# Seven products in another order, with part of their factors' sums and two weight differences moved between them

## The chip, the core and the metric

The kernel runs on one core of one Trainium2 chip. TensorE does the matrix products into PSUM, VectorE, ScalarE and GpSimd do elementwise work, SyncE starts the DMA transfers; each engine works through its own queue in order and waits on semaphores. The metric is the device time of one execution in microseconds (us): 636.19 before, the median of 3 runs (636.09 to 636.86). The profiled execution spans 634.8 us.

## The reference

Two blocks follow one another. The first is a linear attention with a decaying state, the second a two-layer network with SiLU. Cut to what matters:

```python
# r, k, v, w: (4, 8, 768, 48); u: (8, 48)
for t in range(768):
    cur = u * k_t (outer) v_t
    y[:, :, t] = r_t @ (state + cur)
    state = w_t[..., None] * state + k_t (outer) v_t
x = y.transpose(0, 2, 1, 3).reshape(3072, 384)
h = x @ w_in                       # 384 -> 2048
out = (h * sigmoid(h)) @ w_out     # 2048 -> 384
```

All is float32 to the last, with the weights given in 64 bits and rounded on the chip.

## The kernel before

The 3072 tokens are 12 units of 256: 128 time steps of two batches at once. A unit goes through three stages. *Attention*: the decays are multiplied up over seven levels; at each level TensorE makes scores (`score_products`, L669), VectorE writes them into `score` through a mask (`keep_masked`, L679) and grows the queries (L607, L737), GpSimd the keys (L625, L634). The diagonal blocks of 8 steps are made apart: GpSimd multiplies (`block_bonus`, L487), VectorE sums (`block_sum`, L521), two transfers through DRAM turn them round (`block_move`), ScalarE copies them (`block_spread`, L548 and L550), VectorE shuffles (L551) and writes them into `score` (`block_write`, L557). *Up*: eight steps, each two products of 128 x 256 (`up`, L925) and one SiLU into `gt` (L934). *Down*: the second layer.

From unit 1 on the down stage is a Strassen product in its Winograd form. The result of a unit is cut into four quarters c11, c12, c21, c22 (batch by half of the 384 columns), the inner dimension of 2048 into two halves. Seven products of 128 x 1024 by 1024 x 192 (`quarter`, eight chunks each, L991) take the place of eight. Their left factors are `gt` itself or one of four sums s1 to s4 of quarters of `gt` (`sums`, L973, four pieces m = 0 to 3, four instructions each, into `quarters`, which lies in `temps`). Their right factors are quarters of w_out or one of four differences, made once for all units (`weight_sums`, L965: t1, t2, t3 in `own`, and b12 overwritten in `w_out_sb`). Each product ends in a PSUM tile `p_o`, of which there are two in turn; ScalarE copies the first (L998), VectorE adds each of the others to what is known (L1000), into `partial` (u1 to u4) or into the result (`ob`, whose first half lies in `temps`), and SyncE stores a batch of rows once both its halves are there.

The order of the work is written out by hand: the order of the calls is the order in each engine's queue. In the loop over i = 3 to 11, `mix(i)` gives thirteen groups of attention work of unit i (with the start of unit i + 1), and between them stand the steps of `downs(i - 2)` and `ups(i - 1)`, so many after each group as `ROOM` says: one product after each of the first three groups, two after the fourth, two after the fifth, then the up products. In the units after 3 the first three groups are nearly or wholly empty, so the seven products follow one another closely on TensorE, while VectorE and GpSimd work on the block sums, the keys and the queries. `sums` stands behind the up steps 5, 6 and 7. A product two places on needs the PSUM tile of this one, and so the add behind it.

Group 9 (from 0) of unit 3 holds the end of its scores, and in it `block_spread`, whose last instruction is VectorE's shuffle; group 10 holds what leads over to the next unit.

Of the kernel before, what the change touches and what calls it, by code (L numbers as in the profile page):

```python
# [15 lines left out]
ALU = mybir.AluOpType  # L16
# [22 lines left out]
def kernel(  # L39
# [11 lines left out]
    nc = tc.nc  # L51
# [271 lines left out]
    first = {}  # L323
# [10 lines left out]
    for b in range(NB):  # L334
        for x in range(2):
            nc.vector.tensor_single_scalar(out=own_mask[:, b, :, x:x + 1], in_=first[0], scalar=tok[:, x, b:b + 1],
                                           op=ALU.is_equal)
# [113 lines left out]
    at = 768  # L451
# [4 lines left out]
    block_both = spare[:, at:at + NB * H * BLK].rearrange("p (b h s) -> p b h s", b=NB, h=H)  # L456
# [89 lines left out]
    def block_spread(i):  # L546
        flat = block_both.rearrange("p b h s -> p b (h s)")
        nc.scalar.copy(out=flat[:, 0], in_=block_diag[0])  # L548
        for g in range(4):
            nc.scalar.copy(out=flat[(3 - g) * 32:(4 - g) * 32, 1], in_=block_diag[1][g * 32:(g + 1) * 32])  # L550
        nc.vector.stream_shuffle(out=flat[:, 1], in_=flat[:, 1], mask=list(range(31, -1, -1)))  # L551

    def block_write(i):

        shape = [128, NB, NP, L // BLK, BLK]
        for e in range(2):
            nc.vector.copy_predicated(out=score[:, i % NSC, e].rearrange("p (b q) (i s) -> p b q i s", b=NB, s=BLK),  # L557
                                      mask=block_mask[:, :, None].to_broadcast(shape),
                                      data=block_both[:, :, e::2][:, :, :, None, :].to_broadcast(shape))
# [301 lines left out]
    def both(fn, i, *args):  # L861
        return [(fn, i, b, *args) for b in range(NB)]
# [4 lines left out]
    def mix(i):  # L867

        first, second, later = i == NPAIR, i == NPAIR + 1, i > NPAIR
        ahead = i + 1 < len(units)  # L870

        def at(now, *steps):
            return steps if now else ()

        def bonus_steps(j, *steps):
            return [(block_bonus, j, x) for x in steps]

        def sum_steps(j, *steps):
            return [(block_sum, j, x) for x in steps]

        def turns(j):
            return [*both(turn, j, "w"), (product, j, 0), *both(turn, j, "k"), *both(turn, j, "r"), (grow_own, j, 0)]

        def start(j):
            return [*[(product, j, l) for l in range(1, NL)], (grow_own, j, 1)]

        early = bonus_steps(i + 1, 0, 1, 2, 3)
        middle = [*sum_steps(i + 1, 0, 1), *bonus_steps(i + 1, 4, 5)]
        move = [*sum_steps(i, 3, 4), (block_move, i), *at(ahead, (load_rk, i + 1))]
        groups = [[*at(first, *both(turn, i, "w"), (product, i, 0))],  # L890
                  [*at(first, *both(turn, i, "k"), *both(turn, i, "r"), (grow_own, i, 0))],
                  [*at(first, *start(i)), *at(second, *sum_steps(i, 0, 1), *bonus_steps(i, 4, 5))],
                  [(odd_keys, i, 2), (grow_keys, i, 2, False), (grow_queries, i, 2), *at(later, *sum_steps(i, 2))],
                  [(prepare, i, 3), *at(first, *bonus_steps(i, 0, 1, 2, 3)), *at(later, *bonus_steps(i, 6, 7))],
                  [(burst, i, 3), (keep_level, i, 3), *at(first, *sum_steps(i, 0, 1), *bonus_steps(i, 4, 5)), *at(later, *move)],
                  [(keep_level, i, 4), (go_on, i, 4), *at(first, (make_block_mask,), *sum_steps(i, 2), *bonus_steps(i, 6))],
                  [(prepare, i, 5), (reverse_v, i), *at(first, *bonus_steps(i, 7))],
                  [*at(first, *move), *at(later, (block_spread, i), (block_write, i))],
                  [(burst, i, 5), (keep_level, i, 5), *at(first, (block_spread, i)), (keep_level, i, 6), (go_on, i, 6),
                   *at(first, (block_write, i))],  # L900
                  [*at(later and ahead, *early)],
                  [*at(i < len(units) - NB, *both(turn_k, i)), *at(ahead, *turns(i + 1))],
                  [*both(y_state, i), *both(y, i), *both(update, i), *at(ahead, *start(i + 1)), *at(first, *early),
                   *at(later and ahead, *middle), (move_x, i)]]

        loads = block_loads(i + NSLOT) if i + NSLOT < len(units) else []
        if i + 1 < len(units):
            loads.insert(len(loads) // 2, (load_values, i + 1))

        behind = groups[3 if i > NTOK + 1 else 10:]  # L910
        for at, group in enumerate(behind):
            group += loads[at * len(loads) // len(behind):(at + 1) * len(loads) // len(behind)]
        return groups
# [3 lines left out]
    FH, DH = FC // 2, DM // 2  # L917
# [46 lines left out]
        out, one, two = ((t1, b12, b11), (t2, b22, t1), (t3, b22, b12), (b12, b21, t2))[which]  # L964
        nc.vector.tensor_tensor(out=out, in0=one, in1=two, op=ALU.subtract)  # L965

    def sums(i, m):

        lower, upper = (gt[i, x].rearrange("p a (b t) -> p b a t", b=NB) for x in (m, m + FH // 2))
        s1, s2, s3, s4 = (quarters[:, x, 2 * m:2 * m + 2, :] for x in range(4))  # L970
        for out, one, two, op in ((s1, lower[:, 1], upper[:, 1], ALU.add), (s2, s1, lower[:, 0], ALU.subtract),
                                  (s3, lower[:, 0], lower[:, 1], ALU.subtract), (s4, upper[:, 0], s2, ALU.subtract)):
            nc.vector.tensor_tensor(out=out, in0=one, in1=two, op=op)  # L973

    ob, partial = {}, {}
# [1 line left out]
    def quarter(i, which):  # L977

        n, b0 = units[i]

        def g(b, half):
            return lambda f: gt[i, (f + half * FH) // 2][:, f % 2, b * L:(b + 1) * L]

        def s(x):
            return lambda f: quarters[:, x, f, :]

        p = second[0].tile([128, DH], F32, name="p_o", bufs=2)

        left, right = ((g(0, 0), b11), (g(0, 1), b21), (s(1), t2), (s(2), t3), (s(0), t1), (g(1, 1), b12), (s(3), b22))[which]
        for f in range(FH):  # L990
            nc.tensor.matmul(p, lhsT=left(f), rhs=right[:, f, :], start=(f == 0), stop=(f == FH - 1))  # L991
        if which == 0:
            ob[i] = [out_room(b) for b in range(NB)]
            partial[i] = pt.tile([128, 4, DH], F32, name="partial", bufs=1)
        c11, c12, c21, c22 = (ob[i][x][:, y * DH:(y + 1) * DH] for x in range(2) for y in range(2))
        u1, u2, u3, u4 = (partial[i][:, x, :] for x in range(4))
        if which == 0:
            nc.scalar.copy(out=u1, in_=p)  # L998
        for to, known in ((), ((c11, u1),), ((u2, u1),), ((u3, u2),), ((c22, u3), (u4, u2)), ((c21, u3),), ((c12, u4),))[which]:
            nc.vector.tensor_tensor(out=to, in0=p, in1=known, op=ALU.add)  # L1000
        if which >= 5:
            b = 6 - which
            row0 = (b0 + b) * S + n * L
            nc.sync.dma_start(out=out[row0:row0 + L, :], in_=ob[i][b])

    def ups(i):

        steps = [[(up, i, m)] for m in range(FC // 2)]
        for m in range(FH // 2 - 1):

            steps[FH // 2 + 1 + m].append((sums, i, m))
        steps[-1].append((sums, i, FH // 2 - 1))
        return steps

    def downs(i):
        return [[(quarter, i, x)] for x in range(7)]

    def do(*steps):
        for fn, *args in steps:
            fn(*args)  # L1020
# [54 lines left out]
    for m in range(6):  # L1075
# [3 lines left out]

    blocks = block_loads(4)  # L1080
    do(*blocks[0:2], (level, 2, 2), (prepare, 2, 3), (weight_sums, 1), (down, 0, 1, 0), (down, 0, 0, 3), (down, 0, 1, 1),
       (sums, 1, 0), (bonus, 2, 0), (bonus_sum, 2, 0))
    do(blocks[2], (burst, 2, 3), (keep_level, 2, 3), (keep_level, 2, 4), (go_on, 2, 4), (prepare, 2, 5), (bonus, 2, 1),
       (bonus, 2, 2), (down, 0, 1, 2), (bonus_sum, 2, 1), (load_rk, 3), (load_u,), (sums, 1, 1), *blocks[3:7], (down, 0, 1, 3))
    do((burst, 2, 5), (keep_level, 2, 5), (keep_level, 2, 6), (go_on, 2, 6), (up, 1, 6), (bonus_spread, 2), (bonus_write, 2),
       (load_values, 3), *both(turn_k, 2), (weight_sums, 2), (up, 1, 7), (sums, 1, 2))
    do((sums, 1, 3), *both(y_state, 2), *both(y, 2), *both(update, 2),
       (move_x, 2),
       *blocks[7:])

# [2 lines left out]
    for i in range(3, len(units)):  # L1093
        steps = downs(i - 2) + ups(i - 1)
        groups = mix(i)
        if i == NTOK + 1:

            groups[3].insert(0, (weight_sums, 3))
        for group, room in zip(groups, ROOM):
            do(*group)  # L1100
            for step in steps[:room]:
                do(*step)
            steps = steps[room:]
# [32 lines left out]
```

## Time and profile before

| what | us | where it is from |
|---|---|---|
| time, median of 3 | 636.19 | the runs |
| up products, L925, TensorE busy | 258.1 | groups |
| the seven products, L991, TensorE busy (four groups) | 211.9 | groups |
| factor sums L973, VectorE busy (three largest groups) | 98.7 | groups by form |
| the weight difference L965, each | 2.2 | groups by form |
| adds L1000, each | 0.36 | groups by form |
| block writes L557, each | 1.75 | groups |

The 211.9 are 90.5 + 87.4 + 30.4 + 3.6, the 98.7 are 54.7 + 25.0 + 19.0. The columns of such a group are line, engine, operation, tiles, count, then busy time and mean ns of one, then the engine's idle time just ahead of them and who ended it.

The chain of work that ended last, by engine and line (how much of the span each takes on the path back from the last instruction):

```profile
PE 80%; POOL 9%; DMA 4%; DVE 3%; SPq 2%; issue 1%; ACT 1%; POOLq 0%; DVEq 0%; ACTq 0%
```

From 284.99 us on the pieces of this chain are TensorE's alone, one after the other.

### The profile page before, as it was taken

To read this page: it belongs to the slowest core of one execution; us is meant where nothing else is said; L and a number is where in the kernel's file an instruction comes from. 1 tells how busy PE (TensorE), PEld (TensorE's weight loads), DVE (VectorE), ACT (ScalarE), POOL (GpSimd) and SP (SyncE) were. 2 spreads that over 40 slices of the span, in tenths; PEclk is the share of its full clock that TensorE was granted. 3 is DMA by queue.
4 is the path that set the end of the run, shared out by engine and by line. 5 is a ranking of instruction groups with operands and counts; after the bars stand their busy time and mean duration, and the time that the engine had idled before them with its cause. 6 is when DMAs were issued, how large, how long until landed. Compare 5 with 4: busy or idle time off the path is not lost.

```text
span 634.8 us, 12253 instructions
## 1 busy us (share of the span) xinstructions
PE 620.5 (98%) x4574; PEld 561.6 (88%) x4574; DVE 434.4 (68%) x750; ACT 185.8 (29%) x377; POOL 373.7 (59%) x421
## 2 busy tenths in 40 slices
PE   8999999999888999999999999999999999999997
PEld 7888876889788899899889889989989989989997
DVE  7879779885593696696587596497597587561031
ACT  5798881202310321221221221221131122120120
POOL 6998298569469278478278378468458558500000
PEclk9999999999998999999999999999999999999999
DMA  9966864533353643543443442453353222100000
GB/s 216 290 152 167 190 176 50 112 73 65 81 71 55 128 65 52 126 64 51 111 67 52 110 72 49 96 87 51 79 102 53 47 62 52 34 0 26 26 1 25
DMA packets 203292, 53.75 MB, mean 85 GB/s; under 512 B 186465, under 2 KB 194657, under 8 KB 203233
## 3 DMA queue, kind: packets, MB, share of 16 engines
q1 hardware_dynamic: 201648, 52.39, 40.7%
q10 hardware_dynamic: 1584, 0.59, 0.5%
q8 instruction: 36, 0.59, 0.4%
q14 instruction: 24, 0.19, 0.1%
HBM read 43.67 MB, written 5.31 MB: 77 GB/s over the span
## 4 chain that ended last, share of the span: by engine, by line
PE 80%; POOL 9%; DMA 4%; DVE 3%; SPq 2%; issue 1%; ACT 1%; POOLq 0%; DVEq 0%; ACTq 0%
PE p_h L925 36%; PE p_o L991 27%; PE p_sc L669 4%; PE p_m L807 3%; PE p_m L947 2%; PE p_m L669 2%; PE p_m L794 2%; DMA tokens_w<-in_w_dram 2%; POOL ruk L487 2%; POOL tk L625 2%; POOL tw L408 2%; DMA u_bc<-in_u_dram 1%; POOL tk L634 1%; PE p_m L781 1%; PE p_sc L821 1%
## 5 line engine op out<-in xcount | busy, mean ns | idle before, releaser
L925 PE MATMUL p_h<-xt,w_in_sb 128*128 128x256 f32 x1152 | 258.1, 382 | 0.7 <-POOL tk L649 0.7
L925 PEld LDWEIGHTS p_h<-xt,w_in_sb 128*128 128x128 f32 x1152 | 215.9, 190 | 32.6 <-POOL tk L649 0.9
L934 ACT ACTIVATE gt<-p_h 128x512 f32<-128x512 f32 x90 | 53.6, 596 | 248.2 <-PE p_h L925 248.1
L625 POOL TENSOR_TENSOR tk<-tk,tw 128x256 f32<-128x256 f32 x126 | 86.9, 711 | 60.1 <-ACT tk L595 31.3
L991 PE MATMUL p_o<-own,temps 128*128 128x192 f32 x528 | 90.5, 331 | 5.8 <-DVE temps L1000 3.7
L991 PEld LDWEIGHTS p_o<-own,temps 128*128 128x128 f32 x528 | 87.6, 193 | 7.2 <-DVE temps L1000 4.6
L991 PE MATMUL p_o<-w_out_sb,gt 128*128 128x192 f32 x508 | 87.4, 328 | 0.0
L991 PEld LDWEIGHTS p_o<-w_out_sb,gt 128*128 128x128 f32 x508 | 82.7, 190 | 0.9 <-issue 0.4
L487 POOL TENSOR_TENSOR ruk<-tokens_rk 128x768 f32<-128x768 f32 (+1 forms) x36 | 56.3, 1574 | 39.4 <-DMA tokens_rk<-in_k_dram 28.2
L408 POOL TENSOR_TENSOR tw<-tw 128x256 f32<-128x256 f32 (+6 forms) x83 | 45.0, 542 | 52.2 <-DVE tw L360 48.3
L973 DVE TENSOR_TENSOR temps<-gt 128x256 f32<-128x256 f32 x84 | 54.7, 651 | 18.3 <-ACT gt L934 18.3
L595 ACT COPY tk<-tk 128x256 f32<-128x256 f32 x51 | 20.6, 403 | 101.6 <-POOL tk L625 71.9
L607 DVE TENSOR_TENSOR tr<-tr,tw 128x512 f32<-128x512 f32 x62 | 47.6, 768 | 3.7 <-POOL tk L625 1.1
L679 DVE COPY_PREDICATED score<-mask,p_sc 128x512 f32<-128x512 int8 x60 | 42.1, 753 | 10.9 <-PE p_sc L669 10.0
L669 PEld LDWEIGHTS p_sc<-tr,tk 48*128 48x128 f32 x496 | 30.4, 187 | 10.1 <-issue 6.6
L669 PE MATMUL p_sc<-tr,tk 48*128 48x128 f32 x496 | 36.5, 285 | 0.7 <-POOL tk L625 0.7
L521 DVE TENSOR_REDUCE block_sums<-ruk 128x4 f32<-128x192 f32 (+1 forms) x54 | 27.1, 542 | 7.5 <-POOL ruk L487 7.5
L1000 DVE TENSOR_TENSOR ob<-p_o,partial 128x192 f32<-128x192 f32 x22 | 7.9, 358 | 35.4 <-PE p_o L991 35.4
L1000 DVE TENSOR_TENSOR temps<-p_o,partial 128x192 f32<-128x192 f32 x22 | 7.9, 358 | 34.9 <-PE p_o L991 24.7
L557 DVE COPY_PREDICATED score<-spare 128x1024 f32<-128x1024 int8 x18 | 30.6, 1752 | 0.3
L991 PE MATMUL p_o<-w_out_sb,temps 128*128 128x192 f32 x176 | 30.4, 326 | 0.0
L487 POOL TENSOR_TENSOR tokens_rk<-tokens_rk,tokens_w 128x192 f32<-128x192 f32 (+1 forms) x36 | 29.4, 838 | 1.4
(170 smaller groups left out, 825.9 us busy)
## 6 DMA issues: line engine op xcount, KB each, us to landing
w_out_sb<-in_moe_w_in_dram SPq DMA_DIRECT2D x6, 768.0 KB, 8.1
tokens_rk<-in_r_dram SPq DMA_DIRECT2D x9, 384.0 KB, 4.5
tokens_rk<-in_k_dram SPq DMA_DIRECT2D x9, 384.0 KB, 5.5
tokens_w<-in_w_dram SPq DMA_DIRECT2D x9, 384.0 KB, 6.4
w_out_sb<-in_moe_w_out_dram SPq DMA_DIRECT2D x4, 768.0 KB, 6.8
own<-in_moe_w_out_dram SPq DMA_DIRECT2D x4, 768.0 KB, 5.2
xt<-yt SPq DMA_DIRECT2D x60, 48.0 KB, 2.0
raw<-in_w_dram SPq DMA_DIRECT2D x80, 32.0 KB, 2.4
```

The costliest lines, as they stand in the source:

```text
L408: engine.tensor_tensor(out=up, in0=t[:, :, 0::2], in1=t[:, :, 1::2], op=ALU.mult)
L487: mul = lambda out, one, two: nc.gpsimd.tensor_tensor(out=out, in0=one, in1=two, op=ALU.mult)
L521: add = lambda out, have: nc.vector.tensor_reduce(out=out, in_=have, axis=mybir.AxisListType.X, op=ALU.add)
L557: nc.vector.copy_predicated(out=score[:, i % NSC, e].rearrange("p (b q) (i s) -> p b q i s", b=NB, s=BLK), mask=block_mask[:, :, None].to_ ...
L607: nc.vector.tensor_tensor(out=odd, in0=odd, in1=tw[i][l][:, :, 0::2][:, :, :, None].to_broadcast([128, Q, L >> (l + 1), c]), op=ALU.mult)
L625: nc.gpsimd.tensor_tensor(out=out, in0=have, in1=odd_products(i, l, b, *blocks), op=ALU.mult)
L669: nc.tensor.matmul(bass.AP(tensor=s_p.tensor, offset=s_p.offset, ap=[s_p.ap[0], [apart * L // 2, 2], [1, L // 2]]), lhsT=tk[i][rows, X[l % ...
L679: nc.vector.copy_predicated(out=dst, mask=masks[l][:, :, None].to_broadcast([128, NB, NP, ni, c]), data=sc[e].rearrange("p (b q) (i c) -> ...
L925: nc.tensor.matmul(p_h[:, a, :], lhsT=w_in_sb[:, c, f * 128:(f + 1) * 128], rhs=xt[i][:, c, :], start=(c == 0), stop=(c == KC - 1))
L934: nc.scalar.activation(out=gt[i, m], in_=p_h, func=AF.Silu)
L973: nc.vector.tensor_tensor(out=out, in0=one, in1=two, op=op)
L991: nc.tensor.matmul(p, lhsT=left(f), rhs=right[:, f, :], start=(f == 0), stop=(f == FH - 1))
```

## The change

The products change places: after the two of `gt` itself and the one of s2 come s1, s4, s3 and last `gt` again. In the sums s1 and s2 stay behind the up steps (part 0). The four instructions that make s4 now stand behind the second product (part 1), the four that make s3 behind the third (part 2), since their products come only fifth and sixth. The weight difference t3 moves from the end of unit 2's stage into group 2 of pass 3, and the one that overwrites b12 from the head to the end of group 3. The adds go with the products: the fifth now makes c12 and the sixth two results, so the first batch's rows are stored behind the fifth product. Last, the shuffle moves from `block_spread` into `block_write`, and in unit 3 `block_write` from group 9 into group 10, so that both stand behind the mask writes and the first pair of factor sums. The aim is to ease VectorE's queue at the end of the up stage, and to have work in it done nearer to where it is needed.

```diff
--- before.py
+++ after.py
@@ -548,9 +548,11 @@
         nc.scalar.copy(out=flat[:, 0], in_=block_diag[0])
         for g in range(4):
             nc.scalar.copy(out=flat[(3 - g) * 32:(4 - g) * 32, 1], in_=block_diag[1][g * 32:(g + 1) * 32])
+
+    def block_write(i):
+
+        flat = block_both.rearrange("p b h s -> p b (h s)")
         nc.vector.stream_shuffle(out=flat[:, 1], in_=flat[:, 1], mask=list(range(31, -1, -1)))
-
-    def block_write(i):
 
         shape = [128, NB, NP, L // BLK, BLK]
         for e in range(2):
@@ -896,9 +898,8 @@
                   [(keep_level, i, 4), (go_on, i, 4), *at(first, (make_block_mask,), *sum_steps(i, 2), *bonus_steps(i, 6))],
                   [(prepare, i, 5), (reverse_v, i), *at(first, *bonus_steps(i, 7))],
                   [*at(first, *move), *at(later, (block_spread, i), (block_write, i))],
-                  [(burst, i, 5), (keep_level, i, 5), *at(first, (block_spread, i)), (keep_level, i, 6), (go_on, i, 6),
-                   *at(first, (block_write, i))],
-                  [*at(later and ahead, *early)],
+                  [(burst, i, 5), (keep_level, i, 5), *at(first, (block_spread, i)), (keep_level, i, 6), (go_on, i, 6)],
+                  [*at(later and ahead, *early), *at(first, (block_write, i))],
                   [*at(i < len(units) - NB, *both(turn_k, i)), *at(ahead, *turns(i + 1))],
                   [*both(y_state, i), *both(y, i), *both(update, i), *at(ahead, *start(i + 1)), *at(first, *early),
                    *at(later and ahead, *middle), (move_x, i)]]
@@ -964,12 +965,13 @@
         out, one, two = ((t1, b12, b11), (t2, b22, t1), (t3, b22, b12), (b12, b21, t2))[which]
         nc.vector.tensor_tensor(out=out, in0=one, in1=two, op=ALU.subtract)
 
-    def sums(i, m):
+    def sums(i, m, part):
 
         lower, upper = (gt[i, x].rearrange("p a (b t) -> p b a t", b=NB) for x in (m, m + FH // 2))
         s1, s2, s3, s4 = (quarters[:, x, 2 * m:2 * m + 2, :] for x in range(4))
-        for out, one, two, op in ((s1, lower[:, 1], upper[:, 1], ALU.add), (s2, s1, lower[:, 0], ALU.subtract),
-                                  (s3, lower[:, 0], lower[:, 1], ALU.subtract), (s4, upper[:, 0], s2, ALU.subtract)):
+        steps = ((s1, lower[:, 1], upper[:, 1], ALU.add), (s2, s1, lower[:, 0], ALU.subtract),
+                 (s4, upper[:, 0], s2, ALU.subtract), (s3, lower[:, 0], lower[:, 1], ALU.subtract))
+        for out, one, two, op in (steps[0:2], steps[2:3], steps[3:4])[part]:
             nc.vector.tensor_tensor(out=out, in0=one, in1=two, op=op)
 
     ob, partial = {}, {}
@@ -986,7 +988,7 @@
 
         p = second[0].tile([128, DH], F32, name="p_o", bufs=2)
 
-        left, right = ((g(0, 0), b11), (g(0, 1), b21), (s(1), t2), (s(2), t3), (s(0), t1), (g(1, 1), b12), (s(3), b22))[which]
+        left, right = ((g(0, 0), b11), (g(0, 1), b21), (s(1), t2), (s(0), t1), (s(3), b22), (s(2), t3), (g(1, 1), b12))[which]
         for f in range(FH):
             nc.tensor.matmul(p, lhsT=left(f), rhs=right[:, f, :], start=(f == 0), stop=(f == FH - 1))
         if which == 0:
@@ -996,10 +998,10 @@
         u1, u2, u3, u4 = (partial[i][:, x, :] for x in range(4))
         if which == 0:
             nc.scalar.copy(out=u1, in_=p)
-        for to, known in ((), ((c11, u1),), ((u2, u1),), ((u3, u2),), ((c22, u3), (u4, u2)), ((c21, u3),), ((c12, u4),))[which]:
+        for to, known in ((), ((c11, u1),), ((u2, u1),), ((u4, u2),), ((c12, u4),), ((u3, u2), (c22, u4)), ((c21, u3),))[which]:
             nc.vector.tensor_tensor(out=to, in0=p, in1=known, op=ALU.add)
-        if which >= 5:
-            b = 6 - which
+        if which in (4, 6):
+            b = which // 2 - 2
             row0 = (b0 + b) * S + n * L
             nc.sync.dma_start(out=out[row0:row0 + L, :], in_=ob[i][b])
 
@@ -1008,12 +1010,15 @@
         steps = [[(up, i, m)] for m in range(FC // 2)]
         for m in range(FH // 2 - 1):
 
-            steps[FH // 2 + 1 + m].append((sums, i, m))
-        steps[-1].append((sums, i, FH // 2 - 1))
+            steps[FH // 2 + 1 + m].append((sums, i, m, 0))
+        steps[-1].append((sums, i, FH // 2 - 1, 0))
         return steps
 
     def downs(i):
-        return [[(quarter, i, x)] for x in range(7)]
+        steps = [[(quarter, i, x)] for x in range(7)]
+        for part in 1, 2:
+            steps[part] += [(sums, i, m, part) for m in range(FH // 2)]
+        return steps
 
     def do(*steps):
         for fn, *args in steps:
@@ -1079,12 +1084,12 @@
 
     blocks = block_loads(4)
     do(*blocks[0:2], (level, 2, 2), (prepare, 2, 3), (weight_sums, 1), (down, 0, 1, 0), (down, 0, 0, 3), (down, 0, 1, 1),
-       (sums, 1, 0), (bonus, 2, 0), (bonus_sum, 2, 0))
+       (sums, 1, 0, 0), (bonus, 2, 0), (bonus_sum, 2, 0))
     do(blocks[2], (burst, 2, 3), (keep_level, 2, 3), (keep_level, 2, 4), (go_on, 2, 4), (prepare, 2, 5), (bonus, 2, 1),
-       (bonus, 2, 2), (down, 0, 1, 2), (bonus_sum, 2, 1), (load_rk, 3), (load_u,), (sums, 1, 1), *blocks[3:7], (down, 0, 1, 3))
+       (bonus, 2, 2), (down, 0, 1, 2), (bonus_sum, 2, 1), (load_rk, 3), (load_u,), (sums, 1, 1, 0), *blocks[3:7], (down, 0, 1, 3))
     do((burst, 2, 5), (keep_level, 2, 5), (keep_level, 2, 6), (go_on, 2, 6), (up, 1, 6), (bonus_spread, 2), (bonus_write, 2),
-       (load_values, 3), *both(turn_k, 2), (weight_sums, 2), (up, 1, 7), (sums, 1, 2))
-    do((sums, 1, 3), *both(y_state, 2), *both(y, 2), *both(update, 2),
+       (load_values, 3), *both(turn_k, 2), (up, 1, 7), (sums, 1, 2, 0))
+    do((sums, 1, 3, 0), *both(y_state, 2), *both(y, 2), *both(update, 2),
        (move_x, 2),
        *blocks[7:])
 
@@ -1095,7 +1100,8 @@
         groups = mix(i)
         if i == NTOK + 1:
 
-            groups[3].insert(0, (weight_sums, 3))
+            groups[2].append((weight_sums, 2))
+            groups[3].append((weight_sums, 3))
         for group, room in zip(groups, ROOM):
             do(*group)
             for step in steps[:room]:
```

## Prediction

> **What bounds the kernel now.** I read the busy shares first, then the chain of waits, then TensorE's timeline with its gaps, then VectorE and GpSimd side by side in one late pass. Below, "pass i" is one turn of the loop over i = 3 to 11, counted from the first of its seven products (P0 to P6, L991).
>
> ```profile
> PE 620.5 (98%) x4574; PEld 561.6 (88%) x4574; DVE 434.4 (68%) x750; ACT 185.8 (29%) x377; POOL 373.7 (59%) x421
> ```
>
> TensorE is busy 98% of the span and no matmul is removed, so only its gaps can be won. The table by stage, cut at each P0, says where they are:
>
> ```profile
> 128.01:180.26 52.25, 49.38 (x364) 45.16 (x361) 36.31 (x69) 10.88 (x24) 30.44 (x36) 1.00 0.40 73
> 180.26:235.46 55.20, 51.09 (x365) 46.89 (x361) 39.08 (x66) 10.79 (x24) 39.74 (x43) 0.97 0.48 82
> 333.73:382.47 48.74, 48.74 (x361) 45.29 (x361) 35.99 (x61) 10.78 (x24) 31.89 (x36) 1.00 0.43 77
> ```
>
> The first two numbers are the stage's length and TensorE's busy time. A late pass is pure TensorE, 48.74 us. Pass 3 is 3.5 us longer, pass 4 is 6.45 us longer, pass 5 (49.53) 0.8: 10.75 us in all. That is the most the change can bring. TensorE's timeline names the gaps (in brackets: idle, and who ended it):
>
> ```profile
> 137.35 5.47 PE L991 MATMUL p_o<-own,temps 128*128 128x192 f32 x32 [1.27 <-DVE temps L1000]
> 172.11 1.24 PE L781 MATMUL p_m<-ident,tk 128*128 128x128 f32 x8 [1.60 <-DVE score L679]
> 190.46 2.87 PE L991 MATMUL p_o<-own,temps 128*128 128x192 f32 x16 [2.00 <-DVE temps L1000]
> 195.43 4.55 PE L991 MATMUL p_o<-own,temps 128*128 128x192 f32 x16 [2.10 <-DVE partial L1000]
> ```
>
> p_o has two banks, so P(n+2) starts only when VectorE's add of P(n) (L1000) is out of its in-order queue. The 1.60 is another case: the mask write that frees p_m stands behind the shuffle L551, which idled 4.83 us for a copy that waits for a transfer.
>
> Now pass 7, P0 at 333.66, VectorE:
>
> ```profile
> 331.13 1.25 DVE L973 TENSOR_TENSOR temps<-gt 128x256 f32<-128x256 f32 x1
> 332.42 1.15 DVE L973 TENSOR_TENSOR temps<-temps,gt 128x256 f32<-128x256 f32 x1
> 333.49 0.83 DVE L973 TENSOR_TENSOR temps<-gt 128x256 f32<-128x256 f32 x1
> 335.32 0.42 DVE L973 TENSOR_TENSOR temps<-temps,gt 128x256 f32<-128x256 f32 x1
> ...
> 339.63 0.36 DVE L1000 TENSOR_TENSOR temps<-p_o,partial 128x192 f32<-128x192 f32 x1
> 341.76 0.36 DVE L1000 TENSOR_TENSOR partial<-p_o,partial 128x192 f32<-128x192 f32 x1 [1.77 <-PE p_o L991]
> 342.04 0.91 DVE L607 TENSOR_TENSOR tr<-tr,tw 128x512 f32<-128x512 f32 x1
> 342.87 1.12 DVE L521 TENSOR_REDUCE block_sums<-ruk 128x4 f32<-128x192 f32 x4
> 344.36 0.36 DVE L1000 TENSOR_TENSOR partial<-p_o,partial 128x192 f32<-128x192 f32 x1 [0.37 <-PE p_o L991]
> ```
>
> and GpSimd in the same stretch:
>
> ```profile
> 330.62 2.66 POOL L826 TENSOR_TENSOR state<-state,tw 128x512 f32<-128x512 f32 x2
> 333.25 2.91 POOL L408 TENSOR_TENSOR tw<-tw 128x256 f32<-128x256 f32 x6
> 336.12 1.61 POOL L634 TENSOR_TENSOR tk<-tk,tw 128x256 f32<-128x256 f32 x2
> 339.22 1.96 POOL L487 TENSOR_TENSOR ruk<-tokens_rk 128x384 f32<-128x384 f32 x2 [1.49 <-DVE block_sums L521]
> 341.15 0.59 POOL L487 TENSOR_TENSOR tokens_w<-tokens_w 128x192 f32<-128x192 f32 x1
> 341.81 2.14 POOL L487 TENSOR_TENSOR tokens_rk<-tokens_rk,tokens_w 128x192 f32<-128x192 f32 x3
> 343.91 2.61 POOL L625 TENSOR_TENSOR tk<-tk,tw 128x256 f32<-128x256 f32 x4
> 346.48 1.82 POOL L487 TENSOR_TENSOR spare<-tokens_rk 128x768 f32<-128x768 f32 x1
> ```
>
> The same factor sum L973 takes 0.42 us beside an idle GpSimd, and 1.25, 1.15, 0.83 beside L826 and L408: it ends when the GpSimd instruction ends. The L1000 adds, which read PSUM, take 345 to 359 ns whatever GpSimd does. From 339.22 on GpSimd runs without a gap until after P6.
>
> **The Trainium skill.** "SBUF — State Buffer", Who interferes with whom: a VectorE instruction with two SBUF inputs takes the read port that GpSimd uses, and the later one waits for the whole other instruction; reductions never contend. The trace agrees (1.25 against 0.42; L1000 constant). "VectorE: DVE Perf Modes", the errata section: an fp32 tensor_tensor takes (N+151)/0.96 ns, 424 for N = 256; the trace has 0.42, and 0.34 start to start. "Perfetto Trace Analysis", GPSIMD Engine Instruction: trust start-to-start spacing, so I take 0.65 for an L625 (2.61/4) and 0.6 for the short L487.
>
> **The change, part by part.**
>
> *Removed.* Nothing; every instruction is still there. *Moved:* of 16 factor sums (L973) 8 stay with the up products. The four s4 go behind the add of P1, the four s3 behind the add of P2, both ahead of the adds that free the banks of P2 and P3. In pass 3 two weight differences (L965, 1.7 us apart from contention) come in too, ahead of the same adds.
>
> *Before P0.* VectorE is rid of 1.4 us ahead of the transposes (4 x 0.34) and as much ahead of the state add. In late passes this is hidden: the state add waits for TensorE's update (end at P0) and the first add for P1. It moves GpSimd forward: the transposes start 1.3 us sooner, the state products L826 wait for TensorE at about 330.2, so L487 starts near 337.2 instead of 339.2, the block sums being done by then.
>
> *Shuffle and write in pass 3.* The mask write follows its predecessor at 166.2 and ends by 167.5, before TensorE's L781 is due at 170.5: the 1.60 us goes. The shuffle still waits for the transfer, with one pair of sums and the transposes of the next unit queued behind it; GpSimd waits for those, which costs pass 4, not pass 3.
>
> *Passes 5 to 10, the term that decides.* P1 ends at 338.9 in pass 7's clock, and P5 is due at 346.7. Between them VectorE now has: add 0.3, four s4, add 0.3, four s3, L607, L521 (1.05), add 0.35. Bound below, no contention: 0.3 + 1.36 + 0.3 + 1.36 + 0.65 + 1.05 + 0.35 = 5.4 us, fits into 7.8. But each of the nine two-input instructions meets a running GpSimd instruction. In the alternation at 333 to 335 a sum's cycle is GpSimd's step plus about 0.1, so 0.7 each: eight take 5.6. Step by step: the first s4 waits for the short L487 until 339.7, s4 ends at 342.05, add 342.35, s3 pairs with the four L625 and ends at 345.0; L607 then meets the long L487 (1.82) and ends near 347.1, the reduce at 348.1, the add at 348.4. P5 starts 1.7 us late. If GpSimd stands one instruction later, L607 pairs with the last L625 and the wait is 0.15; one earlier, 2.2. I take 1.7. P4 (due 344.1) is not late, s3 and s4 are in time for P5 and P4. Six passes: 6 x 1.7 = 10.2, less the 0.8 that pass 5 lost before: +9.4.
>
> *Pass 11* has no L826 ahead, so GpSimd is done sooner with the short ones: I get 0.3.
>
> *Pass 3.* TensorE from P0 at 128.0: first add at 133.75 (it stood at 136.94), so the 1.27 goes. Then s4 2.1 beside L408, L607 0.75, weight difference 2.0 with the wait: second add done at 139.25, P4 due at 138.55, 0.75 late. Then s3 2.6, L607 1.0, the other difference 2.2: third add done at 145.35, P5 due at 141.9, 3.45 late. 4.2 against 1.55 before: +2.7 (uncontended: 0.65 to 2.05, no change).
>
> *Pass 4.* Relative to P0 GpSimd is ahead by 2 us, but s4 now meets two 1.8 us L487 before the first block sums; the second add ends 3.4 late, and s3 with L607 adds 2.9: 6.3 against 6.45 before, -0.1 (uncontended 2.35, which would be -4.1).
>
> *Tail.* After 592 GpSimd is idle and VectorE nearly so; moving sums there costs nothing. The order of output rows changes one transfer each; the last is still after P6.
>
> Sum: +2.7 - 1.6 - 0.1 + 9.4 + 0.3 = **+10.7 us, 647**.
>
> **Rivals.**
> 1. *Stalls of the early passes go, late ones stay hidden.* For it: the uncontended sums fit in every late pass with over 2 us to spare. Against: GpSimd's unbroken row. Pass 3 -0.2, L781 -1.6, pass 4 -4.1, pass 5 -0.8: -6.7, 629.5.
> 2. *Lucky pairing.* Late passes lose 0.15: +2.7 - 1.6 - 0.1 + 0.9 - 0.8 + 0.3 = +1.4, 637.6. My margin on GpSimd's position is only 0.1 to 0.2 us, so it is real; but nine pairings must all stay.
> 3. *Worse pairing*, 2.2 a pass and 0.5 more in pass 3: +14.2, 650.4.
>
> **How the numbers follow.** Forecast 0.52, rival 1 0.22, rival 2 0.12, rival 3 0.14. Range: from rival 1's time to somewhat over rival 3's, 630 to 651.5. Within 0.2% (634.9 to 637.5) about half of rival 2 and a little of rival 1: 0.08; faster 0.20; slower 0.72.
>
> **What would show it.** In the changed profile each late pass is about 50.4 us between P0s, with TensorE's gap at P5 put down to the L1000 add of "partial", and L973 showing means well over 0.42 between P1 and P3. L781 has no gap in pass 3. I am wrong if the s3 after P2 run at 0.34 apart, or if GpSimd's row has holes there; then rival 1 holds.

## The result, and the profile after

The change makes the kernel slower: 654.14 us (median of 4, 653.87 to 656.3) against 636.53 (median of 4 runs of the kernel before), a ratio of 1.0284 (95% interval 1.0261 to 1.0308). The forecast was 647.0 with a range of 630.0 to 651.5: the direction was right, but the loss is 17.6 us against 10.7, and the time lies above the range. The profiled execution is the slowest of the four (span 654.5 us, 19.7 more than before).

From the page after, the busy shares of the engines and the chain that ended last:

```profile
PE 627.8 (96%) x4574; PEld 566.8 (87%) x4574; DVE 469.6 (72%) x750; ACT 186.2 (28%) x377; POOL 377.2 (58%) x421
PE 69%; DVE 18%; POOL 4%; issue 4%; DMA 3%; ACT 2%; SPq 0%; POOLq 0%; DVEq 0%; ACTq 0%
```

VectorE holds 18% of the path to the end where it held 3%. TensorE's own waits, of which there had been several kinds, are now nearly one line (engine, line, who ended the wait: us in total, times, longest):

```profile
PE p_o L993 <- DVE partial L1002: 19.9, 10, 3.2
```

L993 and L1002 are the products and the adds, L991 and L1000 before; the sums L973 are now L975, the query growth L607 is L609, the keys L625 are L627, the up products L925 are L926 and their SiLU L934 is L935. The stages, cut at each P0, for passes 3, 4, 7 and 8 (columns as in the prediction):

```profile
128.18:182.61 54.43, 51.23 (x362) 46.94 (x361) 40.62 (x71) 10.64 (x24) 34.64 (x38) 0.97 0.37 70
182.61:237.81 55.20, 50.96 (x364) 46.91 (x361) 43.19 (x62) 10.78 (x24) 38.47 (x40) 0.97 0.48 82
...
341.73:392.70 50.97, 49.02 (x365) 45.27 (x361) 39.78 (x60) 10.87 (x24) 31.72 (x36) 1.00 0.41 74
392.70:445.34 52.64, 50.69 (x364) 46.94 (x360) 39.77 (x60) 10.88 (x24) 31.71 (x36) 0.97 0.40 72
```

Pass 7 was 48.74 and is 50.97. Pass 8 is 1.67 longer still, and its granted clock (third column from the end) is 0.97. All passes beside what was forecast, in us longer than before:

| pass | 3 | 4 | 5 | 6 | 7 | 8 | 9 | 10 | 11 | sum |
|---|---|---|---|---|---|---|---|---|---|---|
| forecast | +1.1 | -0.1 | +0.9 | +1.7 | +1.7 | +1.7 | +1.7 | +1.7 | +0.3 | +10.7 |
| measured | +2.18 | 0.00 | +3.42 | +2.23 | +2.23 | +3.89 | +2.21 | +2.24 | +1.16 | +19.56 |

Ahead of pass 3 it is 0.17 more, and the tail is 0.03 shorter, which makes the 19.7. Now VectorE in pass 7, between the add of P1 and that of P3:

```profile
347.29 0.36 DVE L1002 TENSOR_TENSOR temps<-p_o,partial 128x192 f32<-128x192 f32 x1 [2.22 <-issue]
347.57 2.62 DVE L975 TENSOR_TENSOR temps<-gt,temps 128x256 f32<-128x256 f32 x4
350.11 0.34 DVE L1002 TENSOR_TENSOR partial<-p_o,partial 128x192 f32<-128x192 f32 x1
350.38 2.99 DVE L975 TENSOR_TENSOR temps<-gt 128x256 f32<-128x256 f32 x4
353.29 2.30 DVE L609 TENSOR_TENSOR tr<-tr,tw 128x512 f32<-128x512 f32 x1
355.51 1.12 DVE L521 TENSOR_REDUCE block_sums<-ruk 128x4 f32<-128x192 f32 x4
356.56 0.34 DVE L1002 TENSOR_TENSOR partial<-p_o,partial 128x192 f32<-128x192 f32 x1
```

GpSimd beside it:

```profile
349.87 3.21 POOL L627 TENSOR_TENSOR tk<-tk,tw 128x256 f32<-128x256 f32 x4
353.05 1.99 POOL L487 TENSOR_TENSOR spare<-tokens_rk 128x768 f32<-128x768 f32 x1
```

and TensorE's P5 behind it, in pass 7 and in pass 8:

```profile
356.95 2.87 PE L993 MATMUL p_o<-own,temps 128*128 128x192 f32 x16 [1.96 <-DVE partial L1002]
...
407.92 4.55 PE L993 MATMUL p_o<-own,temps 128*128 128x192 f32 x16 [1.96 <-DVE partial L1002]
```

This is the chain of the prediction: the four s4 take 2.62 and the four s3 2.99 where 1.4 each would do alone; the four L627 are stretched from 2.61 to 3.21; L609 meets the long L487 and takes 2.30 where it took 0.91; the add of P3 ends at 356.90, and P5 starts at 356.95. In pass 8 the same gap is followed by 3.41 us in which TensorE runs at half clock, so the same 16 matmuls take 4.55 instead of 2.87.

### The profile page after: what moved, and what is told of

It is laid out like the page before. It is cut to its first block, busy times and chain, and to the rows that moved or that the text cites. A ratio compares the mean times of both kernels' runs of the same rounds, so it can differ in the third digit from the quotient of the medians.

```text
span 654.5 us, 12253 instructions
## 1 busy us (share of the span) xinstructions
PE 627.8 (96%) x4574; PEld 566.8 (87%) x4574; DVE 469.6 (72%) x750; ACT 186.2 (28%) x377; POOL 377.2 (58%) x421
## 4 chain that ended last, share of the span: by engine, by line
PE 69%; DVE 18%; POOL 4%; issue 4%; DMA 3%; ACT 2%; SPq 0%; POOLq 0%; DVEq 0%; ACTq 0%
PE p_h L926 35%; PE p_o L993 16%; DVE temps L975 7%; PE p_sc L671 4%; DVE tr L609 4%; DVE block_sums L521 3%; PE p_m L809 3%; PE p_m L796 2%; PE p_m L948 2%; PE p_m L671 2%; POOL tk L627 1%; DMA tokens_w<-in_w_dram 1%; DMA raw<-in_k_dram 1%; DVE partial L1002 1%; PE p_m L783 1%
## 5 line engine op out<-in xcount | busy, mean ns | idle before, releaser
L926 PE MATMUL p_h<-xt,w_in_sb 128*128 128x256 f32 x1152 | 258.2, 382 | 1.0 <-POOL tk L651 0.7
L926 PEld LDWEIGHTS p_h<-xt,w_in_sb 128*128 128x128 f32 x1152 | 215.9, 190 | 33.1 <-POOL tk L651 0.9
L627 POOL TENSOR_TENSOR tk<-tk,tw 128x256 f32<-128x256 f32 x126 | 92.8, 757 | 79.7 <-PE p_sc L671 41.1
L935 ACT ACTIVATE gt<-p_h 128x512 f32<-128x512 f32 x90 | 53.6, 596 | 259.4 <-PE p_h L926 259.3
L993 PE MATMUL p_o<-own,temps 128*128 128x192 f32 x528 | 95.1, 339 | 16.8 <-DVE partial L1002 16.8
L993 PEld LDWEIGHTS p_o<-own,temps 128*128 128x128 f32 x528 | 90.5, 198 | 19.4 <-DVE partial L1002 19.4
L993 PE MATMUL p_o<-w_out_sb,gt 128*128 128x192 f32 x508 | 87.6, 329 | 0.0
L993 PEld LDWEIGHTS p_o<-w_out_sb,gt 128*128 128x128 f32 x508 | 83.1, 191 | 0.9 <-issue 0.4
L487 POOL TENSOR_TENSOR ruk<-tokens_rk 128x768 f32<-128x768 f32 (+1 forms) x36 | 52.9, 1481 | 44.7 <-DMA tokens_rk<-in_k_dram 21.2
L975 DVE TENSOR_TENSOR temps<-gt 128x256 f32<-128x256 f32 x84 | 61.6, 763 | 22.2 <-ACT gt L935 22.2
L408 POOL TENSOR_TENSOR tw<-tw 128x256 f32<-128x256 f32 (+6 forms) x83 | 41.7, 503 | 37.8 <-DVE tw L360 33.9
L609 DVE TENSOR_TENSOR tr<-tr,tw 128x512 f32<-128x512 f32 x62 | 55.7, 898 | 3.7 <-POOL tk L627 1.1
L681 DVE COPY_PREDICATED score<-mask,p_sc 128x512 f32<-128x512 int8 x60 | 42.0, 753 | 11.5 <-PE p_sc L671 10.7
L993 PE MATMUL p_o<-w_out_sb,temps 128*128 128x192 f32 x176 | 32.3, 339 | 3.3 <-DVE partial L1002 3.2
L993 PEld LDWEIGHTS p_o<-w_out_sb,temps 128*128 128x128 f32 x176 | 30.5, 199 | 3.9 <-DVE partial L1002 3.9
L636 POOL TENSOR_TENSOR tk<-tk,tw 128x256 f32<-128x256 f32 x36 | 32.8, 932 | 0.5
L487 POOL TENSOR_TENSOR tokens_rk<-tokens_rk,tokens_w 128x192 f32<-128x192 f32 (+1 forms) x36 | 31.0, 881 | 1.4
L1002 DVE TENSOR_TENSOR temps<-p_o,partial 128x192 f32<-128x192 f32 x22 | 7.9, 358 | 31.7 <-PE p_o L993 15.8
```

The costliest lines, as they stand in the source:

```text
L408: engine.tensor_tensor(out=up, in0=t[:, :, 0::2], in1=t[:, :, 1::2], op=ALU.mult)
L487: mul = lambda out, one, two: nc.gpsimd.tensor_tensor(out=out, in0=one, in1=two, op=ALU.mult)
L609: nc.vector.tensor_tensor(out=odd, in0=odd, in1=tw[i][l][:, :, 0::2][:, :, :, None].to_broadcast([128, Q, L >> (l + 1), c]), op=ALU.mult)
L627: nc.gpsimd.tensor_tensor(out=out, in0=have, in1=odd_products(i, l, b, *blocks), op=ALU.mult)
L636: nc.gpsimd.tensor_tensor(out=have, in0=have, in1=odd_products(i, l, b, [2, NP * ni]), op=ALU.mult)
L681: nc.vector.copy_predicated(out=dst, mask=masks[l][:, :, None].to_broadcast([128, NB, NP, ni, c]), data=sc[e].rearrange("p (b q) (i c) -> ...
```

## The experiments

In what follows a "gap" is taken from one matmul's start to the next, less the 0.16 us that lie between two starts when nothing waits, so that P5's gap in pass 7 reads 2.12 (1.96 in the brackets of the lines above).

**The order alone** (e1_order: the kernel before, with the new order, its adds and its stores; of the edit the order is shown).

```diff
-((g(0, 0), b11), (g(0, 1), b21), (s(1), t2), (s(2), t3), (s(0), t1), (g(1, 1), b12), (s(3), b22))
+((g(0, 0), b11), (g(0, 1), b21), (s(1), t2), (s(0), t1), (s(3), b22), (s(2), t3), (g(1, 1), b12))
```

> The kernel before with the products in the new order and the adds and stores that go with it, nothing else moved. If the loss comes from sums that meet GpSimd between P1 and P5, the order by itself costs nothing: late passes 48.7 us, all in all 636.5 within 1. If the new order itself is to blame (the adds, two results behind P5, the store behind P4), most of the 17 us is here: 645 to 654.

636.24 us, ratio 1.0004 (0.9996 to 1.0012); passes 6 to 9 are 48.74, without a gap. The order costs nothing.

**The shuffle and write alone** (e2_shuffle, on the kernel before; the shuffle's own move, as in the change, is not shown).

```diff
-[(burst, i, 5), (keep_level, i, 5), *at(first, (block_spread, i)), (keep_level, i, 6), (go_on, i, 6),
- *at(first, (block_write, i))],
-[*at(later and ahead, *early)],
+[(burst, i, 5), (keep_level, i, 5), *at(first, (block_spread, i)), (keep_level, i, 6), (go_on, i, 6)],
+[*at(later and ahead, *early), *at(first, (block_write, i))],
```

> The kernel before with the shuffle and write of the block sums moved, nothing else. The 1.60 us ahead of L781 in pass 3 goes. The transposes of the next unit come some 3 us sooner on VectorE, so GpSimd is sooner in pass 4 too and its 6.4 us of stalls shrink by up to as much again: 632 to 635. Rival: pass 4 waits for GpSimd at the same absolute time, and the 1.6 is given back there: 636.5.

636.37 us, 1.0007 (0.9997 to 1.0017). Pass 3 is 50.85 (it was 52.25), pass 4 53.52 (55.20), pass 5 53.72 (49.53). Both savings are there and are given back one pass later than the rival said: in pass 5 a gap of 3.2, with 3.4 us of half clock behind it.

**s3 back behind the up steps** (e3_s3_back, on the changed kernel, as are the next ones).

```diff
-            steps[FH // 2 + 1 + m].append((sums, i, m, 0))
-        steps[-1].append((sums, i, FH // 2 - 1, 0))
+            steps[FH // 2 + 1 + m] += [(sums, i, m, x) for x in (0, 2)]
+        steps[-1] += [(sums, i, FH // 2 - 1, x) for x in (0, 2)]
...
-        for part in 1, 2:
-            steps[part] += [(sums, i, m, part) for m in range(FH // 2)]
+        steps[1] += [(sums, i, m, 1) for m in range(FH // 2)]
```

> The changed kernel with s3 back behind the up steps; s4 stays behind P1. If the add of P3 is late because s3 and L609 stand ahead of it and take turns with GpSimd, it is now in time: no gap at P5 in passes 6 to 11, stages of 48.7 us, and 631 to 638 in all. If the order, the weight differences or the shuffle are to blame, over 645.

635.53 us, 0.999 (0.9984 to 0.9997). There is no gap in passes 6 to 11, which are as long as before (48.74, and 47.15 for 10 and 11). VectorE in pass 7 (P0 at 332.34):

```profile
341.57 0.82 DVE L609 TENSOR_TENSOR tr<-tr,tw 128x512 f32<-128x512 f32 x1
...
343.35 0.34 DVE L1002 TENSOR_TENSOR partial<-p_o,partial 128x192 f32<-128x192 f32 x1
```

The add of P3 comes 11.0 us after P0 instead of 14.8. Taking the four s3 away from this place undoes the whole loss.

**s4 back, s3 left where the change puts it** (e4_s4_back: the same edit with 0 and 1 in the up steps, part 2 behind P2).

> The changed kernel with s4 back behind the up steps; s3 stays behind P2. If it is only the amount of work between P1 and P5, half of the sums are gone and so is most of the gap (0 to 0.5 us a pass, 637 to 642). If it is the taking of turns, GpSimd, held up less by s4, reaches its long product (L487, 1.8 us) sooner, one of the s3 or L609 meets it all the same, and the gap at P5 stays at 1.5 to 2.2 us in passes 5 to 10: 647 to 653.

640.16 us, 1.0064 (1.0048 to 1.008), gaps at P5 of 0.45 to 0.79 in passes 6 to 10. That is the number of the first reading, a little over its 0 to 0.5, and I had the second one for mine. VectorE in pass 7:

```profile
341.16 3.11 DVE L975 TENSOR_TENSOR temps<-gt 128x256 f32<-128x256 f32 x4
344.19 1.13 DVE L609 TENSOR_TENSOR tr<-tr,tw 128x512 f32<-128x512 f32 x1
```

and GpSimd's long product:

```profile
345.78 1.81 POOL L487 TENSOR_TENSOR spare<-tokens_rk 128x768 f32<-128x768 f32 x1
```

The s3 are as slow as ever (3.11 for four), so they do take turns; but L609 is done in 1.13, since GpSimd reached its long L487 only at 345.78. I had expected it sooner. With the s4 back ahead of them, VectorE comes later to the first block sums, and GpSimd waits 1.49 us for these. So this run does not tell the two readings apart by its time. The next two do.

**Without the long L487** (e6_no_long, bonus step 6).

```diff
-        else:
+        elif step == 7:
             e = step - 6
```

> The changed kernel without the multiply of block bonus step 6 (GpSimd's 1.8 us L487 behind the four L627), so part of the scores is left out. If the query growth L609 behind s3 takes 2.30 us because it stands beside just that instruction, it now takes 0.7 to 0.9 and the gap at P5 falls from 2.1 to 0.5 to 0.8 in passes 5 to 10: 642 to 646. If the gap comes from VectorE's own work or from the adds, it stays at 2 and the time at 652 or more.

643.31 us, 1.0103 (1.0082 to 1.0124); P5's gap is 0.49 to 0.50 in passes 6 to 10 (2.12 with it), and none in pass 11. VectorE in pass 7:

```profile
350.25 0.68 DVE L609 TENSOR_TENSOR tr<-tr,tw 128x512 f32<-128x512 f32 x1
```

One GpSimd instruction that meets one VectorE instruction is worth 1.6 us of each of passes 6 to 10: L609 takes 0.68 and not 2.30, and the gap is 0.50 and not 2.12.

**Without bonus steps 4 to 7** (e9_no_blocks). VectorE's queue keeps its instructions and their order; only GpSimd has less to do.

```diff
+        elif step >= 4:
+            pass
         elif step == 4:
```

> The changed kernel without the multiplies of block bonus steps 4 to 7 (GpSimd's L487 between P0 and P6), so part of the scores is left out; VectorE's queue is the same to the instruction. If the loss is the taking of turns with GpSimd, the sums between P1 and P5 fall to 0.34 apart wherever GpSimd has nothing to do, the gap at P5 is gone and late passes are 48.7 to 49.0: 632 to 640. If it is the amount of work in VectorE's queue, the gap stays over 1 us and the time over 645.

634.84 us, 0.9974 (0.9962 to 0.9986), no gap from pass 5 on. VectorE in pass 7 (two lines further down in this kernel: L977 are the sums, L611 the query growth):

```profile
338.67 1.89 DVE L977 TENSOR_TENSOR temps<-gt,temps 128x256 f32<-128x256 f32 x4
...
341.21 1.42 DVE L977 TENSOR_TENSOR temps<-gt 128x256 f32<-128x256 f32 x4
342.55 0.69 DVE L611 TENSOR_TENSOR tr<-tr,tw 128x512 f32<-128x512 f32 x1
```

and the last that GpSimd does there (its next instruction comes after 349):

```profile
336.66 2.61 POOL L629 TENSOR_TENSOR tk<-tk,tw 128x256 f32<-128x256 f32 x4 [0.52 <-ACT tk L599]
```

The s3, now beside an idle GpSimd, take 1.42. So it isn't the amount of work in VectorE's queue: the same instructions fit once GpSimd is out of the way. Pass 3 keeps its gap of 2.9 here. GpSimd's keys, which were left in, and the weight differences still stand in it; this run does not tell them apart.

**The sums and the order alone** (e7_sums_only: weight differences and shuffle at their old places; of the edit the weight differences in pass 3 are shown).

```diff
-            groups[2].append((weight_sums, 2))
-            groups[3].append((weight_sums, 3))
+            groups[3].insert(0, (weight_sums, 3))
```

> The changed kernel with the two weight differences and the shuffle and write at their places of before: only the order and the sums are moved. If the sums are the cause, passes 6 to 11 are as in the changed kernel (51.0, gap 2.1), and all in all 650 to 656. If the two weight differences in pass 3 cost what I worked out (some 3 us), pass 3 is shorter by that. If it is the pieces left out here that cost, under 642.

655.22 us, 1.0304 (1.0271 to 1.0337), no less than the whole change. P5's gap in pass 3 is 3.24 against 2.93: the weight difference that moved into pass 3 does not lengthen it. So the sums with the order carry the loss, and by the first run the order is free.

**A version to beat both** (e10_best). All sums back behind the up steps, the rest of the change kept, and in pass 4 the block sums, which wait for GpSimd, behind the adds of P2 and P3 and no longer ahead of them (`...` marks what is cut):

```diff
-[*at(first, *start(i)), *at(second, *sum_steps(i, 0, 1), *bonus_steps(i, 4, 5))],
-[(odd_keys, i, 2), ..., *at(later, *sum_steps(i, 2))],
-[(prepare, i, 3), ..., *at(later, *bonus_steps(i, 6, 7))],
+[*at(first, *start(i))],
+[(odd_keys, i, 2), ..., *at(later and not second, *sum_steps(i, 2))],
+[(prepare, i, 3), ..., *at(second, *sum_steps(i, 0, 1), *bonus_steps(i, 4, 5), *sum_steps(i, 2)), *at(later, *bonus_steps(i, 6, 7))],
```

> A version to beat both: the changed kernel with s3 and s4 back behind the up steps, and in pass 4 alone the block sums 0 to 2 and bonus steps 4 and 5 moved behind the fifth product's place (group 4), so that the adds of P2 and P3 don't stand behind sums that wait for GpSimd. Late passes 48.7; pass 4 falls from 55.2 to 49 to 51; 630 to 633. Rival: GpSimd and the transfers are the bound there, pass 5 gives it back, and 635 to 637.

635.43 us, 0.9988 (0.998 to 0.9996): the rival. Pass 4's products lose only 0.6, but its up steps stop once and pass 5 loses 2.1. TensorE in pass 4, at the up step that stops:

```profile
217.53 7.13 PE L926 MATMUL p_h<-xt,w_in_sb 128*128 128x256 f32 x24 [2.43 <-ACT gt L935]
```

VectorE's last block sum of this pass:

```profile
203.78 0.95 DVE L521 TENSOR_REDUCE block_sums<-ruk 128x16 f32<-128x768 f32 x1 [0.82 <-POOL ruk L487]
```

and SyncE's issues (start, then how long they took; `raw` are the loads for a later unit, L540 is the first transfer of the block sums):

```profile
208.97 1.95 SPq L109 DMA_DIRECT2D raw<-in_w_dram  x4
...
211.51 0.38 SPq L540 DMA_DIRECT2D kept<-block_sums  x1
```

VectorE had the block sums ready at 204.7, but their transfer stood in SyncE's queue behind raw loads until 211.5. ScalarE stood in `block_spread` for it, with the SiLU behind, and TensorE behind that.

**The loads of pass 3 spread.** Three kernels with this line changed: e11_loads (e10_best with it), e12_before_loads (the kernel before with it) and e13_e5_loads (the changed kernel with all sums back and with it).

```diff
-        behind = groups[3 if i > NTOK + 1 else 10:]
+        behind = groups[3:]
```

> e10_best with the loads of pass 3 spread from group 3 on, as in the later passes, and no longer all behind group 10. If pass 4 and 5 wait because SyncE works through these 48 issues (0.49 us each) before it can issue the block sums' transfer, that transfer goes out some 5 us sooner in pass 4, the 2.4 us gap at the up step and the 2.1 us at pass 5 shrink, passes 4 and 5 are 49 to 51: 630 to 633. Rival: the chain through GpSimd sets it, and the time stays at 635.4.

e11_loads: 633.15 us, **0.995 (0.9937 to 0.9962)**, the fastest of all and ahead of both kernels, at the upper end of what I had expected. Passes 4 and 5 fall to 48.75, without a gap. What is left is in pass 3, 56.39, where the loads now stand ahead of that pass's transfer. First the line of pass 4, then TensorE in pass 3:

```profile
184.22:232.96 48.74, 48.74 (x364) 45.29 (x360) 34.09 (x61) 10.77 (x24) 35.69 (x41) 1.00 0.42 76
```

```profile
174.07 5.49 PE L926 MATMUL p_h<-xt,w_in_sb 128*128 128x256 f32 x12 [3.94 <-ACT gt L935]
```

> The kernel before with that one line changed. If SyncE's queue holds up the early passes there too, 632 to 635; pass 4's stalls come from adds behind block sums that wait for GpSimd, so most of them stay. Rival: nothing, 636.1.

e12_before_loads: 639.13 us, 1.0045 (1.0032 to 1.0059). On the kernel before the same line costs, since pass 3 grows to 58.09 and pass 4 keeps 3.3 us of gaps. I had expected a gain. In pass 3 TensorE now waits 4.73 us, where it waited 1.60, for the mask write that stands behind the shuffle:

```profile
175.62 1.94 PE L781 MATMUL p_m<-ident,tk 128*128 128x128 f32 x8 [4.73 <-DVE score L679]
```

> e11_loads without the move of pass 4's block steps into group 4: the changed kernel with all sums behind the up steps, and the loads spread. If the adds of pass 4 behind the waiting block sums cost on their own, it is 2 to 4 us over e11_loads: 633 to 636. If the loads are all that counts, the same as e11_loads.

e13_e5_loads: 635.52 us, 0.9992 (0.9986 to 0.9999), 2.4 over e11_loads: that is pass 4, 51.14 against 48.74, and so what the block sums ahead of the adds cost there.

**The loads from group 8 on** (e11_loads with 8 for the 3, in pass 3 alone).

> e11_loads with the loads of pass 3 from group 8 on, so behind the issue of the block sums' transfer in that pass, and spread over five groups where e10_best has three. If SyncE's queue is what makes the block copies late, pass 3 falls from 56.4 to 49 to 50.5, passes 4 and 5 stay under 50.5, and all in all 626 to 630. Rival: what is saved in pass 3 comes back in pass 4, where the last loads now stand ahead of the transfer, as in e10_best: 632 to 635.

636.2 us, 1.0002 (0.999 to 1.0014): the rival, and a little above its 632 to 635. Pass 3 falls to 50.33 as hoped, and passes 4 and 5 (51.26 and 54.32) take it back. How pass 3 could be had as well is open.

## Why the prediction was wrong, by its own steps

*The step that decides* named the right wait, the right place and the right partner: P5 waits for the add of P3, behind s3 and L609, which meet GpSimd, and L609 meets the long L487. e3, e6 and e9 show it. Its size was off: the term "1.7 a pass" measured 2.2. I had let P1 end at 338.9, 5.24 after P0; the modelled end of its matmuls is 5.47 after P0, and the add began at 5.56, 0.3 later than I had it. The four s3 took 2.99 and not 2.65, L609 2.30 and not 2.1; the s4 were a little faster than I had them. In all 0.5 a pass, 2.6 us over passes 6 to 10 without the half clock of pass 8. I had also read that a sum "ends when the GpSimd instruction ends". In both traces a 128x256 sum ends 0.28 us after the one it met (before: L826 at 332.10, the sum at 332.38), and L609, with 512 columns, 0.55 after it (after: L487 at 355.04, L609 at 355.59).

*Left out: the half clock.* The prediction put it at nothing. Behind a gap of 2.1 us or more TensorE sometimes works 3.41 us at half clock, which costs 1.67 (pass 8 against pass 7). The trace of before has one such stretch behind a gap, in pass 4, and I read its 4.55 us group without asking why 16 matmuls took so long. The changed kernel's profile has four, in passes 3, 4, 5 and 8: three more, 5.0 of the 19.6 us. Of the 8.9 us by which the profiled passes exceed the forecast these are 5.0, the mis-sized 1.7 is 2.6, and passes 3, 4, 5 and 11 hold the other 1.2, some with a plus and some with a minus. For the median of the runs the share is open. e7's four runs follow the clock: 652.95 and 653.91 us at a mean granted clock of 0.997, 656.53 at 0.992, 658.93 at 0.989. But the changed kernel's do not: 653.87, 654.01 and 654.28 at 0.991, 0.995 and 0.990, 656.3 at 0.989. And e7 at 0.997, the clock of the profile of before, still loses about 17 us, so its loss is not made by half clock alone. The Trainium skill, "TensorE: Matmul & The Clock Gate", Part 1, gives the window as 4096 cycles at 1.2 GHz, which is the 3.41 seen here. It puts the drop after an idle window of about 3.4 us; here 1.96 us of idle (a gap of 2.12) sufficed at times, and at other times did not. The last section has what the traces show of when.

*Pass 5* was taken for a late pass, +0.9: 3.42, with a gap of 2.4 and one half-clock stretch. *Pass 11*: 1.16 for 0.3. I had GpSimd done sooner with its short instructions; L609 did take 0.68 there, but the eight sums took 6.2 us (2.95 and 3.22), as they met running instructions all the same.

*Pass 3*: the 1.60 ahead of L781 went, as forecast (0.28 for ScalarE is left at the next up step). The rest I charged in good part to two weight differences that come in. Only one does: the one that overwrites b12 stood between the adds of P2 and P3 before as well (at 138.12). And e7 shows that the one that came in does not lengthen the gap (3.24 without it, 2.93 with it); where all sums are behind the up steps the pass has no gap at P5 with both differences in it (e10_best). Of the 2.18 that the pass lost, one half-clock stretch is 1.67.

*Pass 4*: -0.1 forecast, 0.00 measured, and that is luck. The forecast had 3.4 from the add of P2 and 2.9 from s3 with L609. The trace has gaps of 3.35 and 1.22, and 1.67 of half clock that the forecast did not know. The first part, with the two s4 that meet a long L487 each (2.03 us each), was right.

*The tail*, at nothing, is 60.51 against 60.54.

*The rivals.* The first, that the early stalls go and the late ones stay hidden, is refuted by e7. Its early part was partly right, but e2 and e14 show that such savings move on to a later pass. e11 shows that in e10's kernel SyncE's queue holds up passes 4 and 5; that it is the same queue in e2 and e14 is argued from like rows of their traces, not tested. Of the lucky pairing there is no trace. The third rival had the 2.2 a pass by luck: it put GpSimd one instruction earlier, but L609 met the long L487, as in the forecast.

## What to carry to other kernels

Work that is moved to "where it is needed" lands in front of something: name the instruction behind it in the same queue, and who waits for that one. Price a two-input VectorE instruction not by its own time but by what GpSimd runs beside it, in pairs, and look for the longest partner. And add to each TensorE gap of about 2 us or more the chance of a half-clock stretch, which here nearly doubles its cost.

## What the runs showed of the hardware beyond this

- With VectorE and GpSimd both waiting, they take turns, one instruction each: in late passes four sums take 2.62 to 3.22 us beside a busy GpSimd and 1.42 beside an idle one. GpSimd pays less: four L627 go from 2.61 to 3.21.
- A half-clock stretch depends on where the gap falls. Gaps of the same 2.12 us were followed by one in one of passes 6 to 10 in the changed kernel's profile and in one of them in e7's. In each of the fourteen traces, read from 100 us on, the stretches begin on a fixed beat of 3.41 us: in the changed kernel at 145.37, 196.57, 254.60 and 408.20, which are 15, 17 and 45 beats apart. A beat at full clock with 2.00 us or more of idle in it was followed by a stretch 18 times of 18, one with 1.88 or less never; of four with 1.96 three were and one, in pass 7, was not. So a gap of 3.08 us of idle in pass 3 of e7, 1.43 in one beat and 1.64 in the next, brought no half clock. In five traces the stretch is 6.83 us; there 0.74 us or more of idle lay in its first 3.41. This is a reading of the traces: no run moved a gap against the beat.
